# Storing an intermediate as two float32r parts, and loading the parts in one run in the next stage

## The chip, the cores and the metric

The kernel runs on one core of a Trainium2 chip. The metric is the device time of one execution in microseconds (us). An execution is one launch that does everything from the inputs in HBM to the output in HBM.

## The reference

Three layers follow one another over 8 batches of 576 tokens and 512 features. The first is an attention of 8 heads over keys and values that were averaged in groups of 8. The second is a gated MLP whose gate mixes tokens; it ends in a residual sum, which is the intermediate that this change is about. The third is a mixture of 4 causal attention experts, of which each token takes two.

```python
    # second layer: returns x2
    gated = u * v_s
    return (x + gated @ w_out).astype(np.float32)

    # third layer, for each expert e, on x = x2
        q = x @ wq[e]
        k = x @ wk[e]
        v = x @ wv[e]
        scores = scale * (q @ k.transpose(0, 2, 1))
        ...
        ye = a @ v @ wo[e]
```

## The kernel before, in words

Features lie on the 128 partitions in 4 chunks, and the 576 tokens lie along the free dimension. Every product of float32 values is made of three matmuls in float32r: a value is split into a high part (the value rounded to float32r) and a low part (what is left), and high by high, low by high and high by low are summed in PSUM.

The kernel has two stages. **PhaseA** (the first two layers) handles one batch after the other: `vpart` and `norm` (the gate's half of the MLP), `upart`, `spatial` (the mixing of tokens), and then for each of 4 output chunks f `outp(b, f)`, whose 24 matmuls fill a PSUM tile. Beside `outp` the next batch's probabilities are transposed (`trans`), and then `av` makes that batch's input. The matmul tiles of `vpart`, `upart`, `spatial`, `outp` and half of `av` share one PSUM tag `mm` with two buffers; `trans` has the tag `tr` with one buffer. At the end of `outp` one VectorE add (line 461) writes x2 = PSUM + residual into SBUF, and one DMA on SyncE's queue (line 462) stores it in DRAM.

**PhaseB** (the experts) also goes batch by batch, 18 units to a batch: 9 query tiles `u` for each of two pairs of experts `p`. A unit is `score` (matmuls, a VectorE mask and minimum at line 841, a ScalarE exponential at 844), `scale` (the row's factor: line 855 and the reciprocal at 856 on VectorE, then the product at 860, mostly on GpSimd), and three units later `trans` (transposes at 886 on TensorE, split at 890 and 891). After units 5 and 8 comes `av` (906 to 917). Between units the tables `FIRSTF` (first batch), `FILL` (batches 1 to 6) and `LASTF` (last batch) place other work: `1h` is one of four pieces of the second pair's projection of this batch (`10`, `11` are q, `12`, `13` are k), `0h` the same for the next batch's first pair, `v0` to `v4` the next batch's value projection, `g` its gate, `o0` to `o3` the previous batch's output chunks, and `x0` to `x3` the loads of the next batch's x2.

`load_x` (lines 632 to 645) loads one chunk in float32 into a staging tile `xb`, rounds it on VectorE into the high part `xbh` (line 640), and subtracts to get the low part `xbl` (line 643) and, for the last 64 tokens, a copy of the low part behind the high one (line 644). The subtractions run on GpSimd, but for chunk 3 (chunks 2 and 3 for the first two batches) on VectorE. The tile `xbh` has five buffers, four of which a batch uses; `xbl` has one buffer for all four chunks. It can be written only when the last reader of the batch before, the matmuls of `13`, is done. The staging tile has three buffers and doesn't wait for `13`.

The order on each engine's queue is not quite the order of the text: a planner puts an instruction ahead when, by its own costs, it is ready earlier. The four duplications of k that follow each k projection (`kd`, line 751) go through SyncE's queue too, as do the output stores (line 932).

Of the kernel before, what the change touches and what calls it, by code (L numbers as in the profile page):

```python
# [8 lines left out]
F32 = mybir.dt.float32  # L9
F32R = mybir.dt.float32r  # L10
U32 = mybir.dt.uint32
U64 = mybir.dt.uint64
AF = mybir.ActivationFunctionType
# [3 lines left out]
B, H, S, D = 8, 8, 576, 64  # L17
HS = S // 2
# [23 lines left out]
class PhaseA:  # L42
# [405 lines left out]
    def outp(self, b, f):  # L448
        nc, w = self.nc, self.w
        ps = self.ps.tile([128, 2, 512], F32, tag="mm", name="op", bufs=2)  # L450
        c = slice(f * 128, f * 128 + 128)
        for h in range(2):
            s = slice(h * HS, h * HS + HS)
            o = ps[:, h, :HS]
            for k in range(4):
                gh, gl = self.G[b, k]
                nc.tensor.matmul(o, self.wo[0][:, k, c], gh[:, s], start=k == 0, stop=False)  # L457
                nc.tensor.matmul(o, self.wo[0][:, k, c], gl[:, s], start=False, stop=False)  # L458
                nc.tensor.matmul(o, self.wo[1][:, k, c], gh[:, s], start=False, stop=k == 3)  # L459
        x2 = w.tile([128, 2, HS], F32, name="x2", bufs=4)  # L460
        nc.vector.tensor_add(x2, ps[:, :, :HS], self.X32.pop((b, f)))
        nc.sync.dma_start(self.x2d[b][:, f], x2.rearrange("p a b -> p (a b)"))

    def run(self):
        self.weight_tiles()
# [143 lines left out]
LAG = 3  # L609
ALV = 1  # L610
KDM = 1
XV = (3,)
FILL = (('', '12 10 11', '', '13', 'x0', 'x1', 'o3 o1 x2 x3 o0', '', ''), ('v0', 'v1 00 02', '01 o2', '03', '', '', '', 'v2 v3', 'v4 g'))
FIRSTF = (('10', '11', '12', '13', 'x0', '', 'x1 x2', 'x3', ''), ('v0 00', '', '01 02 v1', '03', '', '', '', 'v2 v3', 'v4 g'))
LASTF = (('', '10 12 11', '', '', '13', '', 'o1', '', 'o0'), ('', '', '', '', '', 'o2', '', '', 'o3'))
XV1 = (2, 3)
SDF = {(0, 0), (0, 1), (0, 5), (0, 8), (1, 0), (1, 2), (1, 7)}
SDL = {(0, 4), (0, 6), (1, 6), (1, 7)}
PRE = 'v0 00 01 02 03 v1 v2 v3 v4 g'
# [3 lines left out]
class PhaseB:  # L623
# [8 lines left out]
    def load_x(self, b, kc):  # L632
        nc, w = self.nc, self.w
        if kc == 0:
            self.X[b] = []
            self.xlt = w.tile([128, 4, S], F32R, tag="qt", name="xbl")
        xh = w.tile([128, 640], F32R, tag="P", name="xbh", bufs=5)
        x = w.tile([128, S], F32, tag="e", name="xb", bufs=3)
        nc.sync.dma_start(x, self.x2d[b][:, kc])
        nc.vector.tensor_copy(xh[:, :S], x)  # L640
        xl = self.xlt[:, kc]
        eng = nc.vector if kc in (XV if b > 1 else XV1) else nc.gpsimd
        eng.tensor_sub(xl, x, xh[:, :S].bitcast(F32))
        eng.tensor_sub(xh[:, S:], x[:, 512:], xh[:, 512:S].bitcast(F32))
        self.X[b].append((xh, xl))

    def consts(self):
# [286 lines left out]
    def run(self):  # L934
# [7 lines left out]
        def item(b, x):  # L942
            if x[0] == "x":
                return [lambda: self.load_x(b + 1, int(x[1]))] if b + 1 < B else []
            if x[0] == "o":
                return [lambda: self.outp(b - 1, int(x[1]))] if b > 0 else []
            if x[0] == "1":
                return [part(b, 1)[int(x[1])]]
            if b + 1 == B:
                return []  # L950
            if x[0] == "0":
                return [part(b + 1, 0)[int(x[1])]]
            if x[0] == "v":
                return [vpart(b + 1)[int(x[1])]]
            return [lambda: self.gate(b + 1)]
# [3 lines left out]
        for k in range(len(units) + LAG + 1):  # L959
# [5 lines left out]
            if k < len(units):  # L965
                for x in (LASTF if b + 1 == B else FILL if b else FIRSTF)[p][u].split():
                    for f in item(b, x):
# [22 lines left out]
@with_exitstack  # L990
def kernel(ctx: ExitStack, tc: tile.TileContext, ins, out):
    dram = ctx.enter_context(tc.tile_pool(name="dram", bufs=1, space=bass.MemoryType.DRAM))
    x2 = [dram.tile([128, 4, S], F32, name=f"x2_{b}") for b in range(B)]
    w = ctx.enter_context(tc.tile_pool(name="w", bufs=1))
    with ExitStack() as c:
        a = PhaseA(c, tc, w, ins, x2)
        a.run()
    with ExitStack() as c:
        PhaseB(c, tc, w, ins, x2, out, a.ident).run()
# [16 lines left out]
```

## Time and profile before

| | us |
|---|---|
| median of 3 runs | 981.26 |
| lowest to highest | 980.27 to 981.61 |
| the profiled execution | 980.73 |
| its span, first to last instruction | 978.9 |

| engine | busy, share of the span |
|---|---|
| TensorE | 94% |
| VectorE | 72% |
| ScalarE | 51% |
| GpSimd | 49% |

The span is what lies between the first and the last instruction; 1.8 us lie around it. Times in the rows count from the start of the span. The second stage's first matmul starts at 590.0 us. A busy TensorE counts the modelled latency of each matmul, so two matmuls one behind the other overlap in the rows; a true stop shows as an idle time with its releaser.

### The profile page before, as it was taken

The numbers are of one execution on the slowest core, as the hardware profiler recorded it, in microseconds if no ns is written. First come the engines' busy times: TensorE is split into PE (matmuls) and PEld (weight loads), VectorE is DVE, ScalarE is ACT, GpSimd is POOL, SyncE is SP. The second block draws the span as 40 slices with busy tenths as digits, with TensorE's granted clock in tenths as the row PEclk, the third lists the DMA queues.
The fourth block names the chain that finished last, engine by engine and source line by source line (L and its number), as shares of the span: only waits on it lengthen the run. The fifth ranks groups of instructions, "written<-read, shape, count | busy, mean of one in ns | idle before, by whom it ended". The sixth has DMA issues, their size and how long they took to land.

```text
span 978.9 us, 18305 instructions
## 1 busy us (share of the span) xinstructions
PE 919.7 (94%) x6488; PEld 866.6 (89%) x6488; DVE 705.1 (72%) x1897; ACT 499.5 (51%) x1253; POOL 481.5 (49%) x664
## 2 busy tenths in 40 slices
PE   4887799999999999999999999799999999999997
PEld 4667689989999899899899999799999999898987
DVE  6998547667567477575676425897979797979785
ACT  3755234243333243342433424576767776767776
POOL 6545848459368276483594350333424252525221
PEclk9797899999999999999999999999999999999999
DMA  9611502302303113023023012323332323322121
GB/s 331 224 34 44 175 25 81 108 24 70 119 11 130 61 53 122 25 82 106 24 73 110 1 62 71 85 58 110 84 105 69 105 74 96 98 71 85 48 61 74
DMA packets 37819, 82.92 MB, mean 85 GB/s; under 512 B 4960, under 2 KB 11104, under 8 KB 36832
## 3 DMA queue, kind: packets, MB, share of 16 engines
q1 hardware_dynamic: 37584, 81.75, 26.8%
q8 instruction: 52, 0.85, 0.4%
q14 instruction: 39, 0.32, 0.1%
q10 hardware_dynamic: 144, 0.00, 0.0%
HBM read 49.23 MB, written 18.87 MB: 70 GB/s over the span
## 4 chain that ended last, share of the span: by engine, by line
PE 56%; DVE 25%; ACT 8%; POOL 6%; issue 4%; DMA 1%; SPq 0%; POOLq 0%; ACTq 0%; DVEq 0%
PE op L457 4%; PE op L458 4%; PE sc L224 3%; PE op L459 3%; PE sp L434 3%; PE sp L432 3%; PE sp L433 3%; DVE vnl L402 3%; PE av L906 3%; ACT pr L844 2%; DVE s L841 2%; DVE vnh L404 2%; DVE bs L388 2%; PE tr L275 2%; DVE pbl L891 2%
## 5 line engine op out<-in xcount | busy, mean ns | idle before, releaser
L860 POOL TENSOR_SCALAR pr<-pr,sm,gw 128x128 f32<-128x128 f32 (+3 forms) x119 | 78.1, 657 | 157.8 <-DVE sm L856 129.4
L844 ACT ACTIVATE pr<-s,sm 128x256 f32<-128x256 f32 (+4 forms) x160 | 83.0, 520 | 42.5 <-DVE sm L841 17.3
L326 POOL TENSOR_TENSOR xu<-x 128x576 f32<-128x576 f32 x28 | 39.2, 1432 | 97.3 <-DVE x L321 85.4
L432 PE MATMUL sp<-wsh,vnh 128*128 128x288 f32 x256 | 79.0, 310 | 5.0 <-ACT vnh L400 5.0
L458 PE MATMUL op<-g,woh 128*128 128x288 f32 x256 | 76.9, 301 | 5.9 <-POOL g L445 5.5
L457 PE MATMUL op<-g,woh 128*128 128x288 f32 x256 | 78.4, 308 | 0.0
L416 PE MATMUL up<-x,wih 128*128 128x288 f32 x256 | 76.8, 300 | 1.3 <-ACT xu L324 1.3
L433 PE MATMUL sp<-wsh,vnl 128*128 128x288 f32 x256 | 77.4, 302 | 0.3 <-DVE vnl L402 0.3
L434 PE MATMUL sp<-wsl,vnh 128*128 128x288 f32 x256 | 77.1, 301 | 0.0
L418 PE MATMUL up<-x,wil 128*128 128x288 f32 x256 | 75.7, 296 | 0.0
L715 PE MATMUL pj<-xbh,wql 128*128 128x288 f32 x256 | 75.5, 295 | 0.0
L713 PE MATMUL pj<-xbh,wqh 128*128 128x288 f32 x256 | 75.5, 295 | 0.0
L714 PE MATMUL pj<-xbl,wqh 128*128 128x288 f32 x256 | 75.5, 295 | 0.0
L417 PE MATMUL up<-x,wih 128*128 128x288 f32 x256 | 75.1, 293 | 0.0
L459 PE MATMUL op<-g,wol 128*128 128x288 f32 x256 | 75.0, 297 | 0.0
L886 PE MATMUL t<-ident,pr 128*128 128x128 f32 x320 | 58.1, 280 | 9.1 <-POOL pr L860 5.7
L276 ACT ACTIVATE pth<-tr 128x640 fp32r<-128x640 f32 (+1 forms) x40 | 26.2, 655 | 79.2 <-PE tr L275 69.7
L224 PE MATMUL sc<-kbd,qt 128*128 128x144 f32 (+1 forms) x320 | 51.5, 310 | 14.0 <-DMA qt<-q_in 8.4
L841 DVE CUSTOM_DVE_ANT_0 s<-s,mk 128x512 f32<-128x512 f32 (+3 forms) x128 | 62.4, 487 | 0.7 <-POOL pr L860 0.3
L891 DVE TENSOR_TENSOR pbl<-t,pbh 128x512 fp32r<-128x512 f32 (+3 forms) x128 | 60.6, 484 | 2.4 <-ACT pbh L890 1.4
L224 PEld LDWEIGHTS sc<-kbd,qt 128*128 128x128 f32 (+1 forms) x320 | 45.2, 195 | 17.8 <-issue 11.6
L906 PE MATMUL av<-pbh,vt 128*128 128x320 f32 (+4 forms) x224 | 55.5, 278 | 2.4 <-ACT pbh L890 2.4
(247 smaller groups left out, 3356.6 us busy)
## 6 DMA issues: line engine op xcount, KB each, us to landing
kraw<-k_in SPq DMA_DIRECT2D x16, 576.0 KB, 3.8
x<-x SPq DMA_DIRECT2D x32, 288.0 KB, 2.1
xb<-x SPq DMA_DIRECT2D x32, 288.0 KB, 2.9
kd<-scr SPq DMA_DIRECT2D x64, 144.0 KB, 2.5
out<-o SPq DMA_DIRECT2D x32, 288.0 KB, 2.2
vraw<-v_in SPq DMA_DIRECT2D x16, 512.0 KB, 3.9
qt<-q_in SPq DMA_DIRECT2D x7, 1152.0 KB, 7.8
st<-w_in_in SPq DMA_DIRECT2D x8, 512.0 KB, 9.0
```

The lines of the kernel that those rows point to most:

```text
L224: nc.tensor.matmul(ps[:m, p // 2, (p % 2) * 144:(p % 2) * 144 + 144], qt[:, p, o:o + m], kbd[:, p, :], start=p % 2 == 0, stop=True, skip_g ...
L432: nc.tensor.matmul(o, vh[:, k, c], self.ws[0][:, k, s], start=k == 0, stop=False)
L433: nc.tensor.matmul(o, vl[:, k, c], self.ws[0][:, k, s], start=False, stop=False)
L434: nc.tensor.matmul(o, vh[:, k, c], self.ws[1][:, k, s], start=False, stop=False)
L457: nc.tensor.matmul(o, self.wo[0][:, k, c], gh[:, s], start=k == 0, stop=False)
L458: nc.tensor.matmul(o, self.wo[0][:, k, c], gl[:, s], start=False, stop=False)
L459: nc.tensor.matmul(o, self.wo[1][:, k, c], gh[:, s], start=False, stop=k == 3)
L841: nc.vector.tensor_tensor_reduce(o, o, self.mk[:, 576 - n:576], -0.125, BIG, OP.add, OP.min, st[:, 0:1])
L844: nc.scalar.activation(pt[:, s], o, AF.Exp, bias=st[:, 0:1], scale=-1.0, accum_out=st[:, 1 + 4 * j:2 + 4 * j])
L860: nc.gpsimd).tensor_scalar(pt[:, :n], pt[:, :n], st[:, 3:4], g, op0=OP.mult, op1=OP.mult)
L891: nc.vector.tensor_sub(d(pl), v, d(ph).bitcast(F32))
L906: nc.tensor.matmul(ps[:, s - lo:], vt[:, j, 2 * p + e].rearrange("p a d -> p (a d)"), t[:, e, j * PTS + s:j * PTS + up], start=j == 0 and ...
```

## The change

In `outp` two float32r tiles, `hi` and `lo`, take the place of one; they share the four buffers that `x2` had. For f below 3 the sum is written back into PSUM; ScalarE copies it, rounded, into `hi`; VectorE subtracts `hi` from it into `lo`. For f = 3 the sum goes into `lo`, and GpSimd makes the subtraction in place. Both parts are stored, so the array in DRAM has twice the size.

`load_x` loses its staging tile and all its VectorE and GpSimd instructions. Three DMAs take their place: the high part, the low part, and the low part's last 64 tokens behind the high part. The tables `FILL` and `FIRSTF` put all four loads right behind `13`.

```diff
-        x2 = w.tile([128, 2, HS], F32, name="x2", bufs=4)
-        nc.vector.tensor_add(x2, ps[:, :, :HS], self.X32.pop((b, f)))
-        nc.sync.dma_start(self.x2d[b][:, f], x2.rearrange("p a b -> p (a b)"))
+        hi, lo = (w.tile([128, 2, HS], F32R, tag="x2", name=n, bufs=4) for n in ("x2h", "x2l"))
+        x = ps[:, :, :HS] if f < 3 else lo.bitcast(F32)
+        nc.vector.tensor_add(x, ps[:, :, :HS], self.X32.pop((b, f)))
+        nc.scalar.activation(hi, x, AF.Copy)
+        (nc.vector if f < 3 else nc.gpsimd).tensor_sub(lo, x, hi.bitcast(F32))
+        for i, t in enumerate((hi, lo)):
+            nc.sync.dma_start(self.x2d[b][:, f, i], t.bitcast(F32).rearrange("p a b -> p (a b)"))
...
-FILL = (('', '12 10 11', '', '13', 'x0', 'x1', 'o3 o1 x2 x3 o0', '', ''), ...
-FIRSTF = (('10', '11', '12', '13', 'x0', '', 'x1 x2', 'x3', ''), ...
+FILL = (('', '12 10 11', '', '13 x0 x1 x2 x3', '', '', 'o3 o1 o0', '', ''), ...
+FIRSTF = (('10', '11', '12', '13 x0 x1 x2 x3', '', '', '', '', ''), ...
...
-        x = w.tile([128, S], F32, tag="e", name="xb", bufs=3)
-        nc.sync.dma_start(x, self.x2d[b][:, kc])
-        nc.vector.tensor_copy(xh[:, :S], x)
         xl = self.xlt[:, kc]
-        eng = nc.vector if kc in (XV if b > 1 else XV1) else nc.gpsimd
-        eng.tensor_sub(xl, x, xh[:, :S].bitcast(F32))
-        eng.tensor_sub(xh[:, S:], x[:, 512:], xh[:, 512:S].bitcast(F32))
+        d = self.x2d[b][:, kc]
+        nc.sync.dma_start(xh[:, :S].bitcast(F32), d[:, 0])
+        nc.sync.dma_start(xl.bitcast(F32), d[:, 1])
+        nc.sync.dma_start(xh[:, S:].bitcast(F32), d[:, 1, 512:])
...
-    x2 = [dram.tile([128, 4, S], F32, name=f"x2_{b}") for b in range(B)]
+    x2 = [dram.tile([128, 4, 2, S], F32, name=f"x2_{b}") for b in range(B)]
```

## Rows read from the trace of the kernel before

**Rows 1.** Busy time by stretch: window, length, each engine (instructions), granted clock, DMA share, GB/s.

```profile
76.00:590.00 514.00, 498.76 (x3453) 467.46 (x3451) 321.00 (x553) 185.52 (x300) 308.90 (x427) 0.98 0.22 72
...
669.00:716.00 47.00, 45.57 (x349) 44.19 (x349) 39.96 (x154) 33.82 (x107) 18.48 (x25) 1.00 0.31 88
```

**Rows 2.** Waits of TensorE, 590 to 979 us: total us, times, longest.

```profile
PE t L886 <- POOL pr L860: 5.7, 10, 0.9
PE op L928 <- DVE scr L911: 4.6, 6, 0.9
```

**Rows 3.** Waits of TensorE, 603 to 623 us, in the second stage's first batch.

```profile
PE t L886 <- DVE pr L860: 2.6, 1, 2.6
```

**Rows 4.** Timeline of VectorE: start us, us, line, out<-in; batch 2, first place.

```profile
705.80 1.48 DVE L640 CAST xbh<-xb 128x576 fp32r<-128x576 f32 x1
...
707.77 0.48 DVE L911 TENSOR_TENSOR scr<-av,scr 64x320 f32<-64x320 f32 x1
```

**Rows 5.** Timeline of ScalarE, same place.

```profile
706.04 0.42 ACT L910 ACTIVATE scr<-av 64x320 f32<-64x320 f32 x1
```

**Rows 6.** Timeline of TensorE: the two stops of that batch, in brackets idle time and releaser.

```profile
708.31 0.39 PE L928 MATMUL op<-ah,wqh 128*128 128x256 f32 x1 [0.75 <-DVE scr L911]
...
714.88 0.66 PE L886 MATMUL t<-ident,pr 128*128 128x128 f32 x4 [0.55 <-POOL pr L860]
```

**Rows 7.** Timeline of GpSimd in that batch.

```profile
701.36 0.77 POOL L860 TENSOR_SCALAR pr<-pr,sm,gw 128x512 f32<-128x512 f32 x1
...
705.55 1.42 POOL L643 TENSOR_TENSOR xbl<-xb,xbh 128x576 fp32r<-128x576 f32 x1
...
713.38 1.44 POOL L860 TENSOR_SCALAR pr<-pr,sm,gw 128x512 f32<-128x512 f32 x1 [0.59 <-DVE sm L856]
```

**Rows 8.** Timeline of VectorE in that batch, second place.

```profile
712.61 0.49 DVE L640 CAST xbh<-xb 128x576 fp32r<-128x576 f32 x1
713.03 0.16 DVE L856 RECIPROCAL sm<-sm 128x1 f32<-128x1 f32 x1
```

**Rows 9.** Timeline of VectorE in the first batch of the second stage.

```profile
612.85 0.54 DVE L860 TENSOR_SCALAR pr<-pr,sm,gw 128x512 f32<-128x512 f32 x1
...
618.97 0.15 DVE L856 RECIPROCAL sm<-sm 128x1 f32<-128x1 f32 x1
...
619.40 1.62 DVE L860 TENSOR_SCALAR pr<-pr,sm,gw 128x512 f32<-128x512 f32 x1
```

**Rows 10.** Timeline of TensorE: end of `13`, first and last chunk of `v0`.

```profile
702.92 0.29 PE L715 MATMUL pj<-xbh,wql 128*128 128x288 f32 x1
...
716.16 0.28 PE L781 MATMUL vp<-wqh,xbh 128*128 128x260 f32 x1
...
717.24 0.29 PE L781 MATMUL vp<-wqh,xbh 128*128 128x260 f32 x1
```

**Rows 11.** Timeline of SyncE's queue: issues, merged.

```profile
704.13 2.38 SPq L751 DMA_DIRECT2D kd<-scr  x4
```

**Rows 12.** DMA issues: out<-in, count, KB each, median us from issue to landing.

```profile
xb<-x SPq DMA_DIRECT2D x32, 288.0 KB, 2.9
...
qt<-q_in SPq DMA_DIRECT2D x7, 1152.0 KB, 7.8
```

**Rows 13.** The view of rows 1, for a stretch in which loads follow one another.

```profile
10.00:24.00 14.00, 9.69 (x42) 8.40 (x42) 11.66 (x22) 6.61 (x34) 11.75 (x24) 1.00 1.07 379
```

**Rows 14.** Timeline of VectorE in the first stage, around `outp(5, 0)`.

```profile
452.78 0.76 DVE L461 TENSOR_TENSOR x<-op,xu 128x576 f32<-128x576 f32 x1 [0.18 <-PE op L459]
...
454.87 0.34 DVE L278 SCALAR_TENSOR_TENSOR ptl<-pth,cm,tr 128x128 fp32r<-128x128 f32 x1
```

**Rows 15.** Timeline of ScalarE there.

```profile
453.52 0.71 ACT L276 ACTIVATE pth<-tr 128x640 fp32r<-128x640 f32 x1 [1.90 <-PE tr L275]
```

**Rows 16.** Timeline of TensorE there: the next transposes.

```profile
455.71 0.71 PE L275 MATMUL tr<-ident,P 128*128 128x128 f32 x5
```

**Rows 17.** Timeline of GpSimd, some us later.

```profile
466.68 1.42 POOL L326 TENSOR_TENSOR xu<-x 128x576 f32<-128x576 f32 x1 [15.97 <-DVE x L321]
```

More of the change, by code (lines that the diff above doesn't have):

```diff
@@ L611 @@
 KDM = 1
-XV = (3,)
-FILL = (('', '12 10 11', '', '13', 'x0', 'x1', 'o3 o1 x2 x3 o0', '', ''), ('v0', 'v1 00 02', '01 o2', '03', '', '', '', 'v2 v3', 'v4 g'))
-FIRSTF = (('10', '11', '12', '13', 'x0', '', 'x1 x2', 'x3', ''), ('v0 00', '', '01 02 v1', '03', '', '', '', 'v2 v3', 'v4 g'))
+FILL = (('', '12 10 11', '', '13 x0 x1 x2 x3', '', '', 'o3 o1 o0', '', ''), ('v0', 'v1 00 02', '01 o2', '03', '', '', '', 'v2 v3', 'v4 g'))
+FIRSTF = (('10', '11', '12', '13 x0 x1 x2 x3', '', '', '', '', ''), ('v0 00', '', '01 02 v1', '03', '', '', '', 'v2 v3', 'v4 g'))
 LASTF = (('', '10 12 11', '', '', '13', '', 'o1', '', 'o0'), ('', '', '', '', '', 'o2', '', '', 'o3'))
-XV1 = (2, 3)
 SDF = {(0, 0), (0, 1), (0, 5), (0, 8), (1, 0), (1, 2), (1, 7)}
```

## The prediction

> **What bounds the kernel now.** I read the stretches first [rows 1]. In both stages TensorE is the bound: it is busy for 498.8 of 514 us in the first, and for 45.6 of 47 us in a batch of the second, at a granted clock of 0.98 to 1.00. VectorE has 40 of those 47 us, GpSimd 18. So work that leaves VectorE or GpSimd is worth only what TensorE waits for them. The view of TensorE's waits gives that for the second stage [rows 2]: 4.6 us in six waits of the output projection on VectorE's line 911, and 5.7 us in ten waits of the transposes on GpSimd's factor (line 860). Six is the number of batches that run by `FILL`. The first batch adds one long wait of 2.6 us on a factor that VectorE computes [rows 3]. The timelines then say why these three are late.
>
> The first place is ahead of `o3`. VectorE has a cast of `load_x` (line 640) that takes 1.48 us, and only after it and one subtraction comes the line 911 that TensorE waits for [rows 4]. That instruction's input from ScalarE was there at 706.46 [rows 5]; it began at 707.77. TensorE idles 0.75 us [rows 6]. The second place is ahead of the transposes at 714.88, an idle time of 0.55 us [rows 6]. GpSimd's factor starts late because the reciprocal it needs stands behind another cast of 0.49 us [rows 8], and it takes 1.44 us where the same shape took 0.77 us at 701.36 [rows 7]. In the first batch the factor on VectorE takes 1.62 us where 0.54 is its time without disturbance [rows 9].
>
> Why one cast takes 1.48 us and another 0.49 is seen by laying the engines over each other: during the long one GpSimd makes a subtraction of `load_x`, from 705.55 to 706.97 [rows 4, 7, 8]. The Trainium skill, in "SBUF — State Buffer", section "Who interferes with whom", says that GpSimd and a VectorE copy or cast in a two-port mode hold a shared pair of ports exclusively, the later one being blocked for the other's whole instruction. The trace agrees here, with 1.48 against 0.49 us. A reader who priced the casts at 0.49 us would return 6 x 0.49 at the first place and 6 x 0.42 at the second, 5.5 us in place of the 7.9 us below.
>
> **The change in the second stage.** It takes away four casts a batch, the subtractions on both engines, and so the overlap of the two.
> - First place: without the cast, line 911 can begin up to 1.48 us earlier, but not before 706.46, its input [rows 4, 5]. That is 1.3 us, more than the 0.75 us of idle time, so all of it comes back: 4.6 us over six batches [rows 2].
> - Second place: the reciprocal can come 0.42 us earlier (at 712.61 in place of 713.03), and the factor takes 0.77 in place of 1.44 us, together 1.1 us against 0.55 us of idle time [rows 6 to 8]. Six such waits are 3.3 us.
> - First batch: the factor can start at the reciprocal's end, 619.12, and take 0.54 us; it ends at 619.66 in place of 621.02 [rows 9]. That returns 1.4 of the 2.6 us [rows 3].
>
> The sum is 4.6 + 3.3 + 1.4 = 9.3 us. What TensorE meets next when it runs 1.3 us a batch ahead isn't in the trace: between nothing and all of the 9.3 us may be taken back. I take 1.5 us, near the lower end, because VectorE gets more than 2 us of slack a batch (four casts of at least 0.49) against TensorE's gain of 1.3.
>
> **The loads.** This is where the change adds a wait. The staging tile let the loads run ahead of `13`; now the low part's single buffer makes them wait for the last matmul of `13`, at 703.2 [rows 10]. From there twelve DMAs with 4 x (288 + 288 + 32) = 2432 KB must land before `v0` of the next batch reads them: the first chunk at 716.16, the last at 717.24 [rows 10], which with the 1.3 us returned is 714.9 and 715.9. On SyncE's queue the text puts them behind the four duplications of k of `13`, which are issued from 704.13 to 706.51 [rows 11], but the planner may take them first, since they need no ScalarE copy. So they start between 703.2 and 706.5. For the run itself there are two prices. Loads behind one another moved 379 GB/s [rows 13]; 2.49 MB then take 6.6 us, and ahead of them a load of 288 KB shows 2.9 - 0.8 = 2.1 us of fixed time [rows 12]. That lands the last chunk between 711.9 and 715.2, in time by 4.0 to 0.7 us. The load of q is slower, 1152 KB in 7.8 us [rows 12]; at that ratio the run takes 16.5 us and is late by 3.8 to 7.1 us. I take the faster price, as the x loads are many DMAs in flight like those of rows 13, while q's load is a single one. Expected cost: nothing, but with little to spare if the duplications go first. Behind the loads stand the output stores, for which nobody waits soon.
>
> The Trainium skill, in "DMA: Bandwidth & Descriptors", section "Anatomy of one DMA — SWDGE (gpsimd) path", fits a DMA as about 2.0 us plus its bytes at 436 GB/s. Added up one DMA after the other, an estimate by that page is 12 x 2.0 + 5.7 = 29.7 us, which would be 17 to 20 us late in each of seven batches and cost over 100 us. The trace speaks against adding the fixed parts: one load of 288 KB in 2.9 us is 102 GB/s and q's is 151 GB/s, so 379 GB/s takes several in flight, with their fixed parts side by side [rows 12, 13].
>
> **The change in the first stage.** Each batch gets three VectorE subtractions (0.76 us each by the add of the same shape [rows 14]), four ScalarE copies (0.71 us or a little less [rows 15]), and one GpSimd subtraction (1.42 us [rows 17]). VectorE is free for 193 of 514 us, ScalarE for 328 [rows 1], so the question is only the place. The add into PSUM in place of SBUF I take at the same 0.76 us. For f below 3 the PSUM buffer is held for 0.76 + 0.71 + 0.76 = 2.2 us rather than 0.76; the same buffer is wanted again one `outp` later, and one lasts about 3 us (452.78 to 455.71 with its transposes [rows 14, 16]), so that fits, by 0.7 us. For f = 3, after which `av` wants the buffers, it is freed by the add as before, and GpSimd is idle for 16 us there [rows 17].
>
> One cost can show. Transposes start at 455.71 and need their PSUM buffer, which VectorE's line 278 leaves at 455.21 [rows 14, 16], 0.5 us of slack. If ScalarE takes the new copy ahead of line 276, that copy ends at 453.54 + 0.06 + 0.71 = 454.3, line 276 at 455.0, and VectorE, with the new subtraction ahead, gets to the end of line 278 at about 456.1: a stop of 0.35 us. If line 276 goes first there is none. The two are ready within 0.02 us of each other (453.52 and 453.54 [rows 14, 15]), so the order is open: 0 to 7 x 0.35 = 2.5 us, and I take 1.0. The casts for the second stage's first batch also leave the first stage; that may return some tenths, which I leave out. The second store of each `outp` is one more issue on a queue with nothing urgent behind it.
>
> **Sum.** 9.3 - 1.5 - 1.0 = 6.8 us less. Against the profiled execution that is 980.73 - 6.8 = 973.9 us; the median of the runs shown is 0.53 us above it, so 974.5 us.
>
> **The rivals.**
> - *The loads come late (slower).* The mechanism: `v0` waits for the last chunk, TensorE stands, and this happens in seven batches. It decides from a run of 12.7 us on (issue at 703.2) or 9.4 us (issue at 706.5). At q's price it costs 3.8 to 7.1 us a batch, 27 to 50 us; less the 6.8 us returned, 1001 to 1024 us. A milder form, 1.5 us late behind the duplications, costs 10.5 us: 985 us. For it: the slack of 0.7 us in the worst order. Against it: rows 13. Chance 0.15, most of it in the milder form.
> - *The stops move (no change).* TensorE, no longer held at the two places, is held a little later by ScalarE or by a chain of the same length, and the first stage pays its 2.5 us. With 6 of 9.3 us taken back: 980.73 - 3.3 + 2.5 = 979.9, as a median 980.5 us. For it: TensorE idles only 3% in any case. Against it: the views show other waits to be few. Chance 0.12.
> - *It doesn't do what it says.* The planner might fill the freed places on VectorE with other work, or issue the loads late on SyncE's queue; that ends in one of the two above.
>
> **How the numbers follow.** The forecast has 0.73, with 971.5 (nothing taken back, no cost: 981.26 - 9.3 = 972.0, and a few tenths from the first stage) to 979. About 0.2%, 2 us, is what a measurement of this kernel can tell from no change. The range of 970.5 to 985 takes in the second rival and the mild form of the first; what is left out is the late loads at q's price and a return beyond the stops counted. Faster 0.74, same 0.11, slower 0.15.
>
> **What would show it.** Right: no wait of line 928 on 911 in the `FILL` batches, factors of 512 columns on GpSimd near 0.8 us, no line 640, and `FILL` batches of the second stage shorter by about a microsecond. Wrong: waits of `v0` (line 781) on a DMA; new waits of line 275 on line 278's result in the first stage beyond 2.5 us, or of `outp` on the subtraction.

## The result and the profile after

The changed kernel takes 968.21 us (median of 4 runs, 967.73 to 970.48) against 981.0 us before (4 runs, 980.27 to 981.61). The ratio is 0.9875, with a 95% interval of 0.9857 to 0.9892: 12.8 us less, nearly twice the 6.8 us that were forecast, and below the range, which began at 970.5 us. The profiled execution has a span of 966.1 us against 978.9.

The stretches of after, read as those of before [rows 1]: window, length, then busy time (instructions) of TensorE, its weight loads, VectorE, ScalarE and GpSimd, granted clock, DMA share, GB/s.

```profile
120.00:590.00 470.00, 465.78 (x3244) 435.71 (x3243) 301.75 (x507) 184.88 (x267) 282.97 (x382) 1.00 0.27 90
...
667.00:712.00 45.00, 44.86 (x349) 44.08 (x348) 36.48 (x148) 33.71 (x106) 12.16 (x19) 1.00 0.42 120
```

The number of TensorE instructions that took 47 us in rows 1, 349, now takes 45. VectorE has 36.5 us of them and GpSimd 12.2, and the DMAs carry 120 GB/s in place of 88. The granted clock of this stretch is 1.00 in both, and that of 120 to 590 us is 1.00 before too. TensorE's waits of after, 590 to 970 us (total us, times, longest), answer to rows 2 and 3:

```profile
PE t L886 <- POOL pr L860: 2.6, 4, 0.9
PE av L906 <- ACT pbh L890: 2.4, 3, 1.0
PE t L886 <- DVE sm L855: 1.4, 1, 1.4
...
PE vp L782 <- DMA xbl<-x: 0.3, 1, 0.3
```

The six waits of line 928 on 911 are gone, and of the ten on GpSimd's factor four are left: three in the second stage's first batch and one in its last, neither of which has a `FILL` table. One short wait on a load has come. The places themselves, in after, in the first batch that has a `FILL` table, on VectorE:

```profile
657.05 0.42 DVE L911 TENSOR_TENSOR scr<-av,scr 64x256 f32<-64x256 f32 x1
657.95 0.42 DVE L917 TENSOR_TENSOR al<-scr,ah 128x256 fp32r<-128x256 f32 x1 [0.48 <-ACT ah L916]
658.41 0.48 DVE L911 TENSOR_TENSOR scr<-av,scr 64x320 f32<-64x320 f32 x1
```

and on GpSimd, the factor of 512 columns:

```profile
663.40 0.78 POOL L860 TENSOR_SCALAR pr<-pr,sm,gw 128x512 f32<-128x512 f32 x1 [0.32 <-ACT o L931]
```

Where VectorE had a cast of 1.48 us between the two lines 911 [rows 4], it now waits for ScalarE, and the factor takes 0.78 in place of 1.44 us [rows 7].

Where the time came from is read by laying the starts of the same matmul side by side, here the first score of a batch (line 827). For batches 2 and 3 before, then after:

```profile
692.48 0.39 PE L827 MATMUL s<-kd,qs 128*128 128x320 f32 x1
...
739.32 0.39 PE L827 MATMUL s<-kd,qs 128*128 128x320 f32 x1
```

```profile
689.13 0.39 PE L827 MATMUL s<-kd,qs 128*128 128x320 f32 x1
...
734.25 0.39 PE L827 MATMUL s<-kd,qs 128*128 128x320 f32 x1
```

The same reading for the whole span, in us:

| part | before | after | difference | forecast |
|---|---|---|---|---|
| up to the second stage's first score | 603.23 | 602.82 | -0.41 | +1.0 |
| its first batch | 42.49 | 41.51 | -0.98 | -1.4 |
| the six `FILL` batches | 281.22 | 270.34 | -10.88 | -7.9, of which 1.5 was to be taken back |
| the last batch, to the start of the last matmul | 47.69 | 47.54 | -0.15 | 0 |
| from there to the end | 4.31 | 3.84 | -0.47 | 0 |

A `FILL` batch took 46.76 to 47.14 us before. After, four of the six take 44.81 to 44.93 us, one 45.12 and one 45.70; in these two a load came late, as the sections on the loads show.

### The profile page after: what moved, and what is told of

It is laid out like the page before. It is cut to its first block, busy times and chain, and to the rows that moved or that the text cites. A ratio compares the mean times of both kernels' runs of the same rounds, so it can differ in the third digit from the quotient of the medians.

```text
span 966.1 us, 18451 instructions
## 1 busy us (share of the span) xinstructions
PE 915.0 (95%) x6488; PEld 864.4 (89%) x6488; DVE 693.1 (72%) x1869; ACT 519.0 (54%) x1285; POOL 447.0 (46%) x628
## 4 chain that ended last, share of the span: by engine, by line
PE 63%; DVE 20%; ACT 6%; POOL 5%; issue 3%; DMA 2%; SPq 1%; POOLq 0%; ACTq 0%; DVEq 0%
PE av L906 4%; PE op L457 4%; PE op L458 4%; PE op L459 3%; PE sp L434 3%; PE sp L432 3%; PE sp L433 3%; PE sc L224 3%; PE t L886 3%; DVE vnl L402 3%; PE pj L715 2%; PE pj L713 2%; PE pj L714 2%; DVE vnh L404 2%; DVE bs L388 2%
## 5 line engine op out<-in xcount | busy, mean ns | idle before, releaser
L860 POOL TENSOR_SCALAR pr<-pr,sm,gw 128x128 f32<-128x128 f32 (+3 forms) x119 | 72.7, 612 | 208.1 <-DVE sm L856 140.9
L400 ACT ACTIVATE vnh<-vg,rs 128x512 fp32r<-128x512 f32 (+1 forms) x40 | 27.3, 717 | 54.9 <-POOL rs L392 43.0
L464 POOL TENSOR_TENSOR x2l<-x2l,x2h 128x576 fp32r<-128x576 f32 x8 | 11.4, 1430 | 97.1 <-ACT x2h L463 97.1
```

## The experiments

The theory was that the gain is VectorE's and GpSimd's freed time at the two places; the rivals, that it is the order of loads and stores, that the first stage takes part, and that the loads decide.

### The tables alone

The kernel before, with the new tables and `load_x` as it was.

```diff
-FILL = (('', '12 10 11', '', '13', 'x0', 'x1', 'o3 o1 x2 x3 o0', '', ''), ...
+FILL = (('', '12 10 11', '', '13 x0 x1 x2 x3', '', '', 'o3 o1 o0', '', ''), ...
...
```

`FIRSTF` is changed likewise.

> The kernel before with nothing but the two tables of the change (the four loads right behind 13; casts and subtractions stay). Theory A, the gain is VectorE's and GpSimd's freed time: little changes, 978 to 984 us, the casts only hold up other instructions than line 911. Rival B, the gain is the order of loads and output stores: about 970 us. Where the casts move away from the two places, line 928 may lose its waits on 911 even under A, but the same time must show up as other waits.

It took 983.74 us, a ratio of 1.004 (1.0027 to 1.0052): slower by 0.4%. A `FILL` batch takes 47.2 us, and the first batch 44.8 in place of 42.5. TensorE's waits, 590 to 985 us:

```profile
PE t L886 <- POOL pr L860: 12.6, 9, 3.4
...
PE op L930 <- DVE al L917: 0.9, 6, 0.2
```

The stop ahead of `o3` has shrunk to 0.2 us, and all of it and more stands ahead of the transposes, which wait for GpSimd's factor: 3.4 us once in the first batch, and 7.6 us in six waits of the `FILL` batches. Put together, the casts and subtractions hold up another instruction; they don't go away. The order by itself is worth nothing.

### The tables of before

The change without its tables, so that the loads stand at units 4, 5 and 6 again.

> The kernel after with the two tables of before (loads at units 4, 5 and 6, the last two behind output stores). Theory A: no casts, so the batch stays near 44.9 us unless the loads come later than the value projection reads them; the planner can take a load as soon as 13 is done, so 966 to 972 us. Rival B: back to about 980 us. If the position alone makes the loads late, line 782 waits on a DMA and the time is 975 us or more.

It took 979.52 us, 0.9991 (0.9982 to 1.0). Here too nothing is left of the gain, for another reason. TensorE's waits, 603 to 990 us:

```profile
PE vp L781 <- DMA xbh<-x: 7.1, 5, 1.9
PE t L886 <- POOL pr L860: 2.6, 4, 0.9
```

TensorE's waits on VectorE and GpSimd are those of after, but for one of 0.9 us, while the value projection waits for its load in five batches, 1.4 us on average. SyncE's queue of this kernel shows why: loads of `x` (642 to 644) stand behind output stores, which wait for ScalarE. First its issues, then its own waits on ScalarE's line 931, 644 to 930 us (7.4 us in after, 644 to 914 us):

```profile
710.26 0.43 SPq L643 DMA_DIRECT2D xbl<-x  x1
713.35 1.50 SPq L932 DMA_DIRECT2D out<-o  x2
...
715.87 0.44 SPq L643 DMA_DIRECT2D xbl<-x  x1
```

```profile
SPq L932 <- ACT o L931: 21.6, 12, 2.9
```

The theory expected 966 to 972 us and was wrong in this; the case set beside it, late loads and 975 us or more, is what came. The planner did not bring these loads forward past the stores that the text puts first. So the removal of the work and the place of the loads are both needed; each alone gives no gain.

### The casts stay, the subtractions go

```diff
-        nc.sync.dma_start(xh[:, :S].bitcast(F32), d[:, 0])
+        x = w.tile([128, S], F32, tag="e", name="xb", bufs=3)
+        nc.sync.dma_start(x, d[:, 0])
+        nc.vector.tensor_copy(xh[:, :S], x)
```

> The kernel after, but the high part goes through the staging tile and the VectorE cast, as before; the GpSimd and VectorE subtractions stay away. If the long cast of 1.48 us comes from GpSimd's subtraction running beside it (the shared pair of ports), the casts are now 0.42 to 0.50 us each, and most of the gain stays: 967 to 971 us. If a cast is long for a reason of its own, one cast of 1.4 us a batch remains and line 928 waits 0.7 us again in each of six batches: 973 us or more.

It took 971.59 us, 0.9911 (0.9896 to 0.9926), 0.6 us above the upper end of what was expected. The casts' view (line, engine, operation, count: minimum/median/maximum in ns):

```profile
L644 DVE CAST xbh<-xb x32: 439/454/461, 513.1 to 884.8; 128x576 fp32r<-128x576 f32 x32
```

Not one of 32 casts takes over 0.46 us; before, one in each `FILL` batch took 1.48 to 1.62 us [rows 4], and each of these six began 0.1 to 0.3 us into a subtraction on GpSimd. Four of the six `FILL` batches take 45.0 to 45.2 us, so four casts of 0.45 us without the subtractions cost 0.2 us in such a batch; casts and subtractions together cost 2.3 us at the same tables (47.2 us with the tables alone, against 44.9). The first batch, the first `FILL` batch and one other lose more (43.2, 46.0 and 45.5 us); why is open.

### The subtractions stay, the casts go

```diff
+        x = w.tile([128, S], F32, tag="e", name="xb", bufs=3)
         nc.sync.dma_start(xh[:, :S].bitcast(F32), d[:, 0])
-        nc.sync.dma_start(xl.bitcast(F32), d[:, 1])
-        nc.sync.dma_start(xh[:, S:].bitcast(F32), d[:, 1, 512:])
+        nc.sync.dma_start(x, d[:, 0])
+        eng = nc.vector if kc == 3 or (b < 2 and kc == 2) else nc.gpsimd
+        eng.tensor_sub(xl, x, xh[:, :S].bitcast(F32))
+        eng.tensor_sub(xh[:, S:], x[:, 512:], xh[:, 512:S].bitcast(F32))
```

> The kernel after, but the low parts are made as before by subtractions from a staged float32 tile (GpSimd, chunk 3 on VectorE), while the high part comes by DMA and no cast is there. What is staged is the high part, so the low part is zero: it is left out of the computation. If the casts are what holds VectorE up, line 928 has no waits and factors on GpSimd of 512 columns are near 0.8 us; GpSimd has 6 us more a batch beside 12 of 45, so 968 to 973 us. If GpSimd's load itself made the stops, they come back: 976 us or more.

It took 976.15 us, 0.9952 (0.9936 to 0.9968), and five of the six `FILL` batches take 46.0 to 46.4 us. The wait of `o3` is back, without any cast. TensorE's waits, 590 to 985 us (lines are 3 further down here):

```profile
PE op L931 <- DVE scr L914: 3.7, 5, 0.7
```

VectorE's and GpSimd's timelines ahead of it:

```profile
706.13 0.42 DVE L914 TENSOR_TENSOR scr<-av,scr 64x256 f32<-64x256 f32 x1
707.04 1.55 DVE L920 TENSOR_TENSOR al<-scr,ah 128x256 fp32r<-128x256 f32 x1 [0.48 <-ACT ah L919]
708.62 0.48 DVE L914 TENSOR_TENSOR scr<-av,scr 64x320 f32<-64x320 f32 x1
```

```profile
706.89 1.42 POOL L646 TENSOR_TENSOR xbl<-xb,xbh 128x576 fp32r<-128x576 f32 x1
```

Now it is `al` that takes 1.55 us, where it took 0.42 us in after. It begins 0.15 us into GpSimd's subtraction and ends 0.28 us behind it. It is so in all five batches. The sixth, of 45.19 us, is the test: there the subtraction waited for its load and began behind `al`, which took 0.42 us, and line 931 has no wait. VectorE, then GpSimd:

```profile
753.08 0.42 DVE L920 TENSOR_TENSOR al<-scr,ah 128x256 fp32r<-128x256 f32 x1 [0.48 <-ACT ah L919]
...
753.94 1.43 POOL L646 TENSOR_TENSOR xbl<-xb,xbh 128x576 fp32r<-128x576 f32 x1 [0.96 <-DMA xbh<-x]
```

So at this place a cast isn't needed for the stop; it was the instruction that happened to meet the subtraction. The stop at the second place did not come back: in the `FILL` batches no transpose waits for GpSimd's factor. The section of the Trainium skill that the prediction named ("SBUF — State Buffer", "Who interferes with whom") has this case apart from the copies: a VectorE instruction with two inputs in SBUF contends with a GpSimd instruction that reads SBUF. The trace agrees, with 1.55 against 0.42 us.

### The subtractions on VectorE

The kernel of the section before, with all subtractions on VectorE.

```diff
-        eng = nc.vector if kc == 3 or (b < 2 and kc == 2) else nc.gpsimd
+        eng = nc.vector
```

> As the kernel in which the subtractions stay (976.15 us, FILL batches of 46.0 us), but all of them on VectorE: 4 x (0.75 + 0.22) = 3.9 us of VectorE a batch, nothing on GpSimd. The low part is again left out of the computation (what is staged is the high part). If the stops come from GpSimd's subtractions holding VectorE's two-input instructions up (al, line 917's, took 1.55 us beside one), no instruction is long and the batches fall to 45.5 us or less: 969 to 973 us. If VectorE's own time is what counts, it is no better than 976 us.

It took 983.51 us, 1.0024 (1.0014 to 1.0033), with `FILL` batches of 46.7 us (one 46.9, one 47.6) and a first batch of 44.8. The expectation of 973 us or less falls, and the other one, VectorE's own time, holds. VectorE's timeline has only short instructions there, but four of them stand between the two lines 914 (911 in before):

```profile
709.17 0.76 DVE L646 TENSOR_TENSOR xbl<-xb,xbh 128x576 fp32r<-128x576 f32 x1
709.85 0.22 DVE L647 TENSOR_TENSOR xbh<-xb,xbh 128x64 fp32r<-128x64 f32 x1
709.98 0.76 DVE L646 TENSOR_TENSOR xbl<-xb,xbh 128x576 fp32r<-128x576 f32 x1
710.65 0.22 DVE L647 TENSOR_TENSOR xbh<-xb,xbh 128x64 fp32r<-128x64 f32 x1
```

Line 931 waits 6.1 us in six batches here, and the transposes of these batches 2.8 us on GpSimd's factor. So it doesn't matter whether VectorE is held by another engine or by work of its own: 1.7 us of subtractions ahead of the second line 914 make the `FILL` batches about as long as the one cast of 1.48 us did before. That the loads' place in the table is what puts them there is not tested by itself.

### Each low part loaded twice

```diff
         nc.sync.dma_start(xl.bitcast(F32), d[:, 1])
+        nc.sync.dma_start(xl.bitcast(F32), d[:, 1])
```

> The changed kernel with each low part loaded twice: 4 x 288 KB more in the run of loads. At the 250 to 380 GB/s that the loads show this is 3.1 to 4.7 us more. If arrival is at the edge, nearly all of it becomes a wait of the value projection in seven batches: 20 to 33 us more, 988 to 1001 us. If the loads had 2 us of slack, 976 to 987 us.

It took 987.39 us, 1.008 (1.0053 to 1.0108), with `FILL` batches of 47.0 to 49.7 us in place of 44.9. TensorE's waits, 590 to 985 us:

```profile
PE vp L783 <- DMA xbl<-x: 13.2, 11, 2.9
```

1152 KB more in the run cost 2.0 to 4.8 us a batch, so the loads have little slack. The lower end of the expectation for loads at the edge is missed by 0.6 us. This is what the rival of the late loads looks like; the change itself stays short of it by less than a microsecond.

### The tails last

If the longer batches of the changed kernel come from late loads, they must go when loads that nobody reads soon stand last. The four loads of the last 64 tokens' low part, which only `v4` reads, stand behind the other eight; a second kernel gives the low part of chunk 0 three buffers of its own besides, so that it can be loaded ahead. Both were run with the changed kernel on one chip.

```diff
-        nc.sync.dma_start(xh[:, S:].bitcast(F32), d[:, 1, 512:])
         self.X[b].append((xh, xl))
+        if kc == 3:
+            for k, (t, _) in enumerate(self.X[b]):
+                nc.sync.dma_start(t[:, S:].bitcast(F32), self.x2d[b][:, k, 1, 512:])
```

```diff
-        xl = self.xlt[:, kc]
+        xl = self.xlt[:, kc] if kc else w.tile([128, S], F32R, tag="e", name="xb0", bufs=3)
```

> The changed kernel once more, beside its two variants on the same chip: 966 to 970 us, FILL batches of 44.9 us, at most two short waits of the value projection on a DMA.

> The changed kernel with the four loads of the last 64 tokens' low part behind the other eight; nobody reads them before v4. If the loads arrive just as the value projection reads them (in the trace of the changed kernel the last low part lands within 0.1 us of its use), the waits on a DMA vanish and the batches of 45.1 and 45.7 us go to 44.9: 0.5 to 1.2 us faster than the changed kernel. If the arrival has slack, no change within 0.2%.

> As the one with the tails last, and in addition the low part of chunk 0 has three buffers of its own, so it is loaded ahead and eleven DMAs are left behind 13. If arrival is the limit, as fast as or up to 0.5 us faster than the one with the tails last; if it is not, the same.

| kernel | median us | ratio to before, 95% interval | `FILL` batches, us |
|---|---|---|---|
| the changed kernel again | 969.74 | 0.9896 (0.9881 to 0.9911) | 44.83 to 45.37 |
| tails last | 967.85 | 0.9872 (0.9856 to 0.9889) | 44.89 to 44.95 |
| tails last, low part of chunk 0 apart | 967.47 | 0.9872 (0.9858 to 0.9887) | 44.88 to 44.93 |

In both variants every `FILL` batch has the length of the changed kernel's best ones, and no wait on a load is left. With the tails last, the last low part lands 0.7 to 1.9 us ahead of its use in the `FILL` batches; in the first profile of the changed kernel it is 0.0 to 0.8, in the second 0.0 to 1.4. So the longer batches were late loads. The medians are 1.9 and 2.3 us lower, where 0.5 to 1.2 and up to 0.5 more were expected. Every one of the eight runs is below every run of the changed kernel beside them, but the changed kernel's first measurement was 0.9875 and the intervals overlap: that the variants are faster in all is likely and not shown.

### No split in the first stage

```diff
-        hi, lo = (w.tile([128, 2, HS], F32R, tag="x2", name=n, bufs=4) for n in ("x2h", "x2l"))
-        x = ps[:, :, :HS] if f < 3 else lo.bitcast(F32)
-        nc.vector.tensor_add(x, ps[:, :, :HS], self.X32.pop((b, f)))
-        nc.scalar.activation(hi, x, AF.Copy)
-        (nc.vector if f < 3 else nc.gpsimd).tensor_sub(lo, x, hi.bitcast(F32))
+        x2 = w.tile([128, 2, HS], F32, name="x2", bufs=4)
+        nc.vector.tensor_add(x2, ps[:, :, :HS], self.X32.pop((b, f)))
+        for i in range(2):
+            nc.sync.dma_start(self.x2d[b][:, f, i], x2.rearrange("p a b -> p (a b)"))
```

> The changed kernel with the first stage of before: one float32 sum per chunk, no ScalarE copy, no subtraction, stored twice (the split is left out of the computation, so the second stage reads twice the sum). It shows what the split costs in the first stage: its batches took 66.88 us before and 67.02 us after. If the split costs that, batches return to 66.9 us and the time falls by about 1 us; if the second DMA store is the cost, they stay at 67.0. The second stage stays at 44.9 us a batch either way.

It took 968.15 us, 0.9872 (0.9856 to 0.9888), no different from the changed kernel within its scatter. The second stage did not stay at 44.9 us a batch: two of its `FILL` batches take 45.5 and 46.5 us, with waits on loads of 0.3 and 1.0 us, so late loads took back what the first stage returned. The batches of the first stage show the cost all the same. For two batches of the kernel before, the start of the same matmul (line 344):

```profile
278.38 0.39 PE L344 MATMUL vp<-wih,x 128*128 128x512 f32 x1
...
345.26 0.39 PE L344 MATMUL vp<-wih,x 128*128 128x512 f32 x1
```

That is 66.88 us. By the same reading the second to sixth batches of after take 67.02 to 67.04 us (one 67.23), and those of the kernel without the split 66.89 to 66.94. From the last of these matmuls to the second stage's first score it is 57.18 us with the split (57.17 when the kernel is run again) and 56.61 without it. So the split costs about 0.1 us a batch and 0.6 us at the end, 1.1 to 1.3 us in all (by the second and the first profile of the changed kernel).

## Why the prediction was wrong, point by point

**What bounds the kernel: right.** TensorE bounds both stages, and the gain is the stops that went, at the places named. After the change TensorE's idle times in all six `FILL` batches together are 0.5 us on VectorE's line 891 and 0.3 us on a load.

**The size of a stop: the step that failed.** The sum took the idle time of the wait view as the stop, 0.75 and 0.55 us a batch. But a matmul in these rows lasts longer than the time after which the next one starts, so the idle time counts from an end that is modelled late. The place in the kernel before, in batch 2, and the same three matmuls in after, in batch 1:

```profile
707.22 0.34 PE L840 MATMUL s<-qs,qzvlo 128*128 128x384 f32 x1
...
708.54 0.28 PE L929 MATMUL op<-ah,wql 128*128 128x256 f32 x1
...
714.05 0.27 PE L840 MATMUL s<-qs,qzvlo 128*128 128x128 f32 x1
```

```profile
659.00 0.34 PE L840 MATMUL s<-qs,qzvlo 128*128 128x384 f32 x1
659.17 0.28 PE L928 MATMUL op<-ah,wqh 128*128 128x256 f32 x1
659.29 0.28 PE L929 MATMUL op<-ah,wql 128*128 128x256 f32 x1
```

From line 840 to 928 it was 1.09 us (707.22 to the 708.31 of rows 6) and is 0.17: the stop was worth 0.92 us, where the row says 0.75. The matmul behind the stop then took 0.23 us to the next start, where it takes 0.12: another 0.11. So this stop cost 1.03 us. Ahead of the second, the time from start to start was 0.83 us (714.05 to the 714.88 of rows 6); in after the same pair has 0.12 us:

```profile
664.60 0.28 PE L840 MATMUL s<-qs,qzvlo 128*128 128x128 f32 x1
664.72 0.62 PE L886 MATMUL t<-ident,pr 128*128 128x128 f32 x4
```

That is 0.71 where the row says 0.55. Together it is 1.74 us a batch in place of 1.30, six times 10.4 us. The rest shows when a whole batch is laid side by side, start by start; the order of the matmuls is the same. Batch 1 took 46.76 us and takes 44.81: 1.84 of the 1.95 us lie at the two stops, in the first matmul behind the first stop, and in the first 320-column matmul of `o3` (0.09 us longer before); what is left lies in steps of less than 0.1 us. The four batches without a late load are 2.0 us below the mean before, so the first two terms of the sum, 4.6 and 3.3 us for six batches, should together have been near 11.9. With it the forecast would have been 970.5 us, at the lower end of its range; most of the rest of the miss lies in the first stage.

**What is taken back: near in size, by luck.** 1.5 us were taken off for waits that TensorE would meet next. On VectorE and GpSimd none came in the `FILL` batches, for the reason given (VectorE gets more slack than TensorE gains), which argued for nothing off. What did take time back are the loads, which the forecast put at nothing: 0.2 and 0.8 us in the batches of 45.12 and 45.70 us. So the six batches are 10.88 us shorter and not 11.9.

**The mechanism at the two places: right in what, short in why.** The prediction took the cast as the thing that holds VectorE up, made long by GpSimd's subtraction. The two experiments that keep one of the two show that the subtraction is the larger part: without it the casts cost 0.2 us in most batches, and without the casts it costs 1.1, against 2.3 for both at these tables. It struck a cast in one kernel and `al`, with two inputs in SBUF, in the other. For the change, which removes both, it makes no difference. The prediction gave no reason why the factor at the second place takes 1.44 us. In the five batches where it does, VectorE's own subtraction of chunk 3 runs inside it:

```profile
713.47 0.74 DVE L643 TENSOR_TENSOR xbl<-xb,xbh 128x576 fp32r<-128x576 f32 x1
```

No run takes this one subtraction alone away, so that it is the cause is likely and not shown.

**The first batch: right in kind, 0.4 us too large.** 1.4 us forecast, 0.98 measured. Its transposes still wait 1.4 us. VectorE's factor ends at 619.47 us, and the chain to it begins with a line 855 at 618.13 that waited 0.62 us for ScalarE's exponential (line 844); the forecast didn't see this chain.

**The first stage: near in size, by another way, then hidden.** The split costs 1.1 to 1.3 us, forecast at 1.0. The feared order of ScalarE's copies didn't come at `outp(5, 0)`: line 276 goes first, and VectorE puts its subtraction between 277 and 278. One `outp` later the copy does go ahead of line 276 (456.16 and 456.71), but no transpose of line 275 waits in the view of this stage, 120 to 590 us.

```profile
452.97 0.71 ACT L276 ACTIVATE pth<-tr 128x640 fp32r<-128x640 f32 x1 [1.90 <-PE tr L275]
453.57 0.65 ACT L463 ACTIVATE x2h<-op 128x576 fp32r<-128x576 f32 x1
```

That the table shows -0.41 in place of +1.0 has two causes. One is the start of the kernel, which scatters from run to run: the same matmul of the first batch (line 344) starts at 68.03 us in one profile of the changed kernel and at 69.39 in the other, and that of the second batch at 143.39 and 145.35. Before, these are 68.75 and 144.67. Up to the first of these matmuls TensorE's order is the same in all three. About 1.3 us of the 12.8 can be of that kind and not the change's. The other is the loads of the second stage's first batch, which are issued from 510 to 528 us, in the first stage. From line 344 of the seventh batch to that of the eighth it is 67.5 us in the two kernels with casts and subtractions, 68.15 and 68.35 in those with subtractions alone, and 66.8 to 66.9 in all others. That returns 0.65 us, the tenths that the prediction left out.

**The loads: the outcome nearly right, the price too low.** The forecast was a landing between 711.9 and 715.2 us for a use at 715.9, so 0.7 to 4.0 us of slack; counted from the end of `13` that is 8.7 to 12.0 us for a use at 12.7. In the `FILL` batches the last low part lands 11.4 to 12.9 us behind the end of `13`, 0.0 to 0.8 us ahead of its use. And this with fewer loads than the twelve of the sum: two are issued ahead of the duplications of k, and two, the high part and the tail of the next batch's first chunk, go a whole batch earlier into the fifth buffer of `xbh` (the issue at 665.53 is such a one; it lands at 670.53, behind the use of this batch's fourth chunk). In the changed kernel, batch 1, the duplications of k, the last low part, the early load, and then the use of the low part (line 782, the fourth chunk):

```profile
655.90 2.53 SPq L751 DMA_DIRECT2D kd<-scr  x4
...
661.58 0.43 SPq L643 DMA_DIRECT2D xbl<-x  x1
...
665.53 0.46 SPq L642 DMA_DIRECT2D xbh<-x  x1
```

```profile
667.18 0.29 PE L782 MATMUL vp<-wqh,xbl 128*128 128x260 f32 x1
```

It has 5.6 us from the start of its issue to its use, and the view of the tile gives

```profile
DMA to landing us min/median/max: 2.9/4.1/5.9
```

so the last ones can arrive as they are read. In two of the six batches TensorE met the edge, in one of them with a wait that the view shows:

```profile
802.76 0.39 PE L782 MATMUL vp<-wqh,xbl 128*128 128x260 f32 x1 [0.33 <-DMA xbl<-x]
```

The kernel that loads the low parts twice shows what the other side of this edge costs. With the loads behind one another, a low part of 288 KB takes 4.1 us to land (median) where a load took 2.9 [rows 12].

**The rivals.** The late loads came in two batches of the changed kernel (45.12 and 45.70 us, the second with 0.3 us of wait in the view), and in full with the old tables. The stops that move came in none, but are what the tables alone produce.

## What to carry to other kernels

Price a stop of TensorE by the time between the starts of the matmuls around it, against the same pair where nothing waits, not by its idle time in the view of waits; here the difference was 0.28 and 0.16 us for idle times of 0.75 and 0.55 us, about a third. Where VectorE is a little late ahead of a bound engine, look first at what GpSimd runs at that moment: a subtraction of 1.42 us there cost VectorE 1.0 to 1.1 us here. And work replaced by loads is only gone if the loads' place is moved too: the new loads at the old places, and the new places with the old work, were each worth nothing.

## What the runs showed of the hardware that was not expected

- A subtraction of 1.42 us on GpSimd stretched a VectorE subtraction with both inputs in SBUF from 0.42 to 1.55 us, and a cast from 0.45 to 1.48. Only the copies had been expected to suffer. A cast of the kernel before that began 0.09 us ahead of such a subtraction (619.05 us) took 0.44.
- TensorE took 0.1 us more than usual from the first matmul behind a stop of 0.9 us to the next (0.23 against 0.12 us), in all six `FILL` batches, at a granted clock of 1.00 in the batch of rows 1.
- The start of the kernel scatters by 1.4 us between two profiles of the same program, while most batches behind it agree within 0.15 us; those that don't, in the second stage, had a late load in one of the two. Small changes are read from the length of a batch, not from the total.
